# A fixed task list replaced by another: threshold attention and a GELU layer on one Trainium2 core

## The chip, the cores and the metric

The kernel runs on one core of a Trainium2 chip. The metric is the device time of one execution in microseconds (us); less is better. The core's engines each run their own queue of instructions in order: PE (matrix products), DVE (VectorE), ACT (ScalarE), POOL (GpSimd) and SP (SyncE, which here only issues transfers). They wait for one another by semaphores.

## The reference

Attention in which a score counts only if it lies within `tau` of its row's maximum, then two dense layers with a sigmoid-weighted activation between them. q, k and v are 8 x 8 x 576 x 64, `x` is 4608 x 512, the weights 512 x 2048 and 2048 x 512. The weights arrive as float64.

```
scores = scale * np.matmul(q, k.transpose(0, 1, 3, 2))
thresh = np.max(scores, axis=-1, keepdims=True) - tau
scores = np.where(scores >= thresh, scores, -1000000000.0)
scores = scores - np.max(scores, axis=-1, keepdims=True)
attn = np.exp(scores)
attn = attn / (np.sum(attn, axis=-1, keepdims=True) + 1e-09)
x = np.matmul(attn, v)            # (B, H, S, D), then as (B*S, H*D)
h = x @ w_in
g = h * (1.0 / (1.0 + np.exp(-1.702 * h)))
return (g @ w_out)
```

## The kernel before, in words

**Attention.** The 64 heads are handled as 32 pairs n. For each pair, scores are 9 pieces of PE work (`scores_run n,[j]`, line 733), which ACT copies to SBUF (`keep n,j`, L750) into 5 tiles, four of 1152 columns and one of 576. DVE finds maxima in groups (`in_groups`, L773; `over_tiles`, L782), ACT and DVE join the halves (`cross_max` L793, `over_halves` L800, `turn_rows` L808/809), and the row goes through DRAM by GpSimd (`row_out` L825, `row_in` L834), which also adds it to some tiles in the transfer itself (`add_row n,t` L840); DVE does it for others (`sub n,t` L855). ACT then runs `mask n,t` (L862) and `exps n,t` (L866). PE multiplies with v (`values n,tiles`, L877; the first pairs' sums also by PE, `sums_by_pe`), DVE and ACT form the sums (`in_groups` again, `cross_sums` L932, `turn_sums` L937 to 941), they go by DRAM (`sums_out`, `sums_in`, L946, L953), and DVE divides and writes the result into x (`place_x n`, L988).

**The layers.** x is taken in 18 blocks of 256 tokens. Block 0's first layer is plain: `mm1_0 j,i` (L1074, j = 0 to 15), `tanh j` on ACT (L1031), `gelu_0 j` on DVE (L1080), the texts' `gelu j`. Its second layer, and both layers of the later blocks, take 7 products of halves instead of 8 (`product blk,x`, L1619; `read`, L1634 and 1641). Block 0's `product 0,0` needs sums of `w_out` that `t_whole` (DVE, L1204) and `t_minus` (ACT, L1200) form after the last weight piece. PE has 40 small fillers, `stay_warm x` (L1685).

**The weights.** 32 pieces of 512 KB, 0 to 15 of `w_in` and 16 to 31 of `w_out`, are sent for by SP (`load_w i`, L651) and converted on the core: `cv_power i` and `cv_power2 i` on ACT (L661, L665), `cv_whole i` and `cv_end i` on DVE (L679, L686). The raw pieces share a few staging places. Piece 28 takes that of 27, piece 29 that of 23, piece 30 that of 24 and piece 31 that of 30: each load waits for the `cv_end` of the piece before it. SP's transfers also use 8 semaphores in turn, so each waits for the landing of the eighth before it.

**What sets the order.** The builder makes 4767 tasks with their dependencies, and then runs them in the order of `ORDER`, a list of 4767 task numbers on lines 290 to 490. The order of one engine's tasks in this list is the order of its queue; the pools (PSUM banks, score places) are taken in it too. `run_in_order` (L492) walks it:

```
for i in map(int, ORDER):
    x_free.extend(x_used.pop(key) for key in x_ends.get(i, ()) if key in x_used)
    tasks[i][3](*tasks[i][4])
```

Of the kernel before, what the change touches and what calls it, by code (L numbers as in the profile page):

```python
# [32 lines left out]
def kernel(  # L33
# [249 lines left out]
    def transfer(by, time, a, kind=0, give=(), lag=1.7):  # L283
# [7 lines left out]
        192 193 199 195 197 200 196 201 198 268 202 270 269 0 271 6 1 205 264 206 207 7 275 208  # L291
        266 209 265 277 211 210 194 214 212 12 267 216 2 213 18 219 13 215 383 217 221 379 4 220
        224 3 19 274 381 222 225 223 226 24 276 384 229 30 8 380 318 36 218 227 287 382 301 230
        308 385 320 25 319 228 323 14 42 289 321 48 315 231 325 324 31 232 328 9 322 330 326 310
        298 329 203 37 317 327 331 333 233 282 280 335 332 386 284 304 334 43 338 336 234 235 295 389
        339 54 15 291 340 49 286 60 32 279 236 66 285 391 303 307 38 281 452 337 204 390 237 341
        26 294 312 454 392 302 342 299 55 46 393 238 343 344 316 395 239 345 394 398 448 61 396 283
        52 346 400 33 5 403 399 40 305 22 401 293 67 405 450 242 27 288 313 404 300 245 408 406
        453 410 243 455 314 64 309 449 34 306 240 248 297 347 451 251 397 20 272 409 358 252 348 10
        411 407 246 459 362 359 35 241 458 402 244 72 273 253 16 412 56 254 249 17 39 255 11 21  # L300
        256 28 247 349 363 250 73 257 352 350 258 355 50 460 259 41 353 260 70 413 261 351 461 311
        414 278 23 354 669 366 415 262 51 78 670 367 84 356 416 665 368 53 79 44 263 90 417 462
        29 96 369 85 667 357 418 464 419 463 420 666 465 467 364 423 469 91 360 370 426 468 371 470
        97 671 361 429 472 421 387 668 372 471 365 373 672 76 473 466 422 474 388 374 88 102 475 375
        376 424 477 479 432 103 478 523 456 82 480 476 425 296 482 435 481 483 427 457 436 484 57 485
        437 428 58 377 438 486 59 439 433 487 488 430 378 489 440 62 675 490 524 431 94 736 676 434
        441 63 738 737 68 443 65 491 442 677 445 739 69 678 45 446 502 492 681 679 444 740 682 100
        683 506 680 503 80 686 741 742 684 292 447 687 688 81 108 691 493 114 689 693 692 696 694 496
        525 494 507 530 499 497 531 695 495 532 743 498 690 510 500 109 511 685 697 512 71 501 115 698
        120 513 504 699 673 746 514 121 508 505 515 83 811 118 674 700 747 47 516 509 112 813 701 702  # L310
        748 518 124 74 703 106 126 749 812 520 92 517 704 75 521 519 814 86 752 750 744 77 127 753
        522 754 116 757 751 755 526 758 807 527 745 756 93 533 705 534 110 809 759 130 535 762 95 716
        760 706 764 808 536 763 767 761 765 720 537 717 104 528 766 105 538 768 529 87 769 111 107 541
        117 707 98 721 539 770 542 99 113 708 540 101 545 771 810 710 132 543 138 718 133 544 144 546
        772 711 89 773 139 709 713 549 774 722 119 775 547 145 817 550 150 723 712 548 884 151 728 553
        551 724 886 719 885 714 552 554 776 727 128 887 715 557 142 787 725 777 555 129 558 726 788 122
        146 148 729 818 123 131 559 136 819 147 125 821 820 560 824 156 822 778 162 157 730 290 888 825
        134 827 781 826 830 890 163 828 154 152 831 556 833 135 823 836 889 832 834 837 137 153 891 839
        160 838 731 842 158 829 843 732 164 561 791 140 733 835 159 779 562 792 166 894 734 840 141 149
        565 958 165 841 735 563 959 789 566 167 564 844 168 161 782 169 569 143 567 155 174 793 845 180  # L320
        175 780 570 568 960 847 783 784 815 181 573 170 795 848 574 961 571 849 962 796 790 816 171 850
        572 851 794 172 577 846 575 964 852 182 963 178 183 173 184 785 965 578 185 576 186 786 798 187
        853 581 176 797 579 864 854 177 582 580 799 865 188 179 585 583 800 190 801 584 189 586 802 191
        803 593 589 868 804 587 594 869 590 866 595 805 867 596 895 806 855 601 602 588 591 603 870 592
        871 607 896 856 604 858 597 608 598 605 609 859 606 599 612 611 857 610 613 999 861 860 600 615
        872 862 873 616 863 614 998 897 618 874 1000 898 900 899 876 903 901 875 904 1001 906 905 877 909
        907 878 910 912 879 911 915 902 913 880 916 918 908 917 619 919 881 617 921 914 922 882 1003 892
        620 968 923 1002 883 924 622 920 893 1004 926 623 1005 621 927 925 625 928 929 930 939 626 624 943
        931 933 628 932 627 936 940 629 934 947 935 636 633 1007 937 637 630 635 944 632 1006 1200 638 634
        640 938 1202 1201 941 948 969 631 1203 942 970 972 975 971 1196 949 973 976 945 978 1197 974 977 981  # L330
        979 946 982 980 984 983 987 985 950 988 951 990 986 989 993 952 994 966 991 953 641 639 995 992
        954 955 996 643 1198 967 1164 642 1165 644 956 1199 1166 1167 647 1168 957 1177 1171 1181 648 1169 1178 1170
        646 1008 1174 650 1172 649 645 1175 651 1182 1185 1173 653 1206 1176 1009 997 1179 1207 1272 1186 1180 1208 1268
        1273 1210 1213 1209 1211 1214 652 1183 1187 1216 1215 1219 1217 1212 1184 1220 1222 1221 1269 1225 1188 1223 1226 1224
        1228 1227 1231 1229 1218 1232 1204 654 1233 1189 1230 1190 656 1270 1205 1234 1236 1274 1191 1237 657 655 1192 1271
        659 1238 1239 1028 1011 1275 658 1249 1240 660 1010 1193 1030 1253 1243 1250 1241 1242 1035 1194 1031 1032 1278 1029
        1195 661 1036 1033 1344 1246 662 1254 1034 1346 1039 663 1244 1038 1247 1041 1012 1257 664 1040 1251 1043 1345 1042
        1248 1045 1235 1245 1255 1258 1279 1252 1280 1282 1281 1285 1283 1259 1013 1256 1286 1288 1287 1284 1291 1289 1292 1347
        1260 1294 1293 1261 1297 1295 1298 1296 1340 1300 1299 1303 1301 1037 1304 1290 1047 1305 1341 1046 1306 1044 1302 1262
        1048 1452 1308 1453 1014 1309 1050 1049 1310 1311 1057 1052 1263 1321 1015 1264 1054 1312 1053 1342 1325 1322 1051 1058  # L340
        1315 1276 1055 1265 1313 1318 1059 1064 1056 1060 1065 1326 1314 1061 1066 1343 1068 1063 1266 1067 1062 1069 1316 1454
        1277 1329 1323 1071 1016 1324 1456 1070 1350 1267 1072 1327 1331 1317 1455 1416 1075 1319 1074 1307 1320 1073 1351 1330
        1352 1354 1353 1357 1355 1328 1017 1358 1360 1359 1332 1363 1361 1333 1364 1362 1366 1365 1457 1369 1367 1356 1334 1370
        1372 1368 1371 1375 1373 1376 1335 1076 1377 1374 1336 1412 1378 1078 1380 1417 1348 1077 1381 1018 1079 1337 1413 1382
        1383 1081 1080 1349 1418 1393 1384 1082 1397 1387 1394 1385 1414 1386 1390 1419 1084 1019 1338 1388 1401 1085 1391 1083
        1389 1087 1103 1086 1398 1392 1105 1402 1395 1415 1104 1110 1396 1020 1106 1107 1399 1089 1111 1400 1339 1108 1090 1109
        1422 1091 1114 1092 1113 1659 1423 1379 1661 1424 1021 1426 1425 1660 1403 1429 1427 1430 1662 1404 1432 1431 1405 1435
        1433 1022 1406 1436 1434 1023 1438 1088 1437 1024 1441 1439 1663 1428 1442 1444 1665 1440 1443 1447 1445 1448 1420 1115
        1664 1446 1116 1449 1666 1112 1450 1118 1627 1117 1421 1407 1628 1093 1120 1094 1119 1629 1630 1408 1095 1631 1640 1122
        1121 1409 1634 1644 1632 1641 1123 1633 1025 1410 1125 1635 1124 1411 1636 1096 1127 1097 1645 1126 1669 1098 1132 1129  # L350
        1637 1731 1099 1128 1648 1735 1130 1133 1638 1670 1131 1134 1732 1451 1671 1135 1736 1673 1639 1136 1676 1138 1139 1733
# [2416 lines left out]
```

## Time and profile before

| what | value |
|---|---|
| median of 3 runs | 1212.37 us (1211.54 to 1212.95) |
| profiled execution | 1211.57 us |
| its span on the core | 1209.5 us, so 2.07 us lie around it |
| busy: PE, DVE, ACT, POOL | 1192.7, 1062.4, 790.0, 131.3 us |
| PE's granted clock | 1.00 in every stretch |
| span up to `product 0,0` on PE | 172.55 us |

Busy times are of the profiled execution, as are all positions below, in us from the start of its span. PE's share of 99% is a mean: up to 172.5 us the attention of the first pairs, the conversion of the weights and block 0's first layer run on all engines at once, and behind it PE has nearly no gap.

### The profile page before, as it was taken

The page shows a single profiled execution, that of the slowest core. Times are in us where ns is not written, and L with a number is a line of the kernel's source. Part 1 is how long each engine was busy: PE and PEld are TensorE (multiplying, and loading weights), DVE is VectorE, ACT ScalarE, POOL GpSimd, SP SyncE. Part 2 cuts the span into 40 slices and gives each one's busy share as a digit, 9 for nine tenths or more (in the row PEclk, how much of TensorE's full clock was granted, in tenths as well). Part 3 has the DMA queues.
Part 4 walks back from the last instruction along what each step waited for, and adds up shares of the span by engine and source line. Part 5 has one row for each costly group of instructions (what it writes and reads, how often), then busy time and mean ns, then how long its engine had stood idle before and what let it go on. Part 6 is the DMA issues. An engine that isn't in the chain of part 4 may idle for free.

```text
span 1209.5 us, 26132 instructions
## 1 busy us (share of the span) xinstructions
PE 1192.7 (99%) x10560; PEld 980.6 (81%) x10560; DVE 1062.4 (88%) x1622; ACT 790.0 (65%) x1183; POOL 131.3 (11%) x176
## 2 busy tenths in 40 slices
PE   8899999999999999999999999999999999999998
PEld 6556777788877777777777777777778999999998
DVE  6999998989899889998898778997886798799797
ACT  7999986878686779678875568667872340340340
POOL 0122232110001110021100110111100000000000
PEclk9999999999999999999999999999999999999999
DMA  9967778696555655557645644557624544454433
GB/s 263 219 144 191 176 140 167 132 173 191 134 130 129 170 129 116 132 141 179 143 94 119 144 112 102 130 120 181 150 71 132 176 148 141 147 154 137 153 118 114
DMA packets 220616, 176.55 MB, mean 146 GB/s; under 512 B 148752, under 2 KB 165776, under 8 KB 220368
## 3 DMA queue, kind: packets, MB, share of 16 engines
q1 hardware_dynamic: 197776, 125.42, 38.5%
q0 software_dynamic: 22032, 49.17, 20.6%
q8 instruction: 83, 1.36, 0.5%
q10 hardware_dynamic: 688, 0.30, 0.1%
q14 instruction: 37, 0.30, 0.1%
HBM read 119.53 MB, written 25.84 MB: 120 GB/s over the span
## 4 chain that ended last, share of the span: by engine, by line
PE 85%; ACT 8%; DVE 3%; DMA 2%; issue 1%; ACTq 0%; POOL 0%; SPq 0%; DVEq 0%
PE ops L1619 23%; PE pv L877 10%; PE ps L733 9%; PE hps L1311 9%; PE ps L1311 7%; PE ops L1575 6%; PE hps L1466 6%; PE ps L1575 5%; PE ps L1466 5%; PE hps L1138 2%; ACT arena L750 2%; PE ps L1138 2%; ACT arena L866 2%; ACT arena L862 2%; DMA arena<-in_moe_w_out_dram 1%; ACT w_in L661 1%
## 5 line engine op out<-in xcount | busy, mean ns | idle before, releaser
L773 DVE TRANSPOSE_TENSOR_REDUCE part<-arena 128x36 f32<-128x1152 f32 (+1 forms) x250 | 294.7, 1209 | 15.7 <-ACT arena L750 9.0
L750 ACT COPY arena<-ps 128x576 f32<-128x576 f32 x288 | 172.2, 646 | 61.5 <-PE ps L733 60.1
L862 ACT ACTIVATE arena<-arena 128x1152 f32<-128x1152 f32 (+1 forms) x160 | 168.5, 1065 | 53.2 <-DVE arena L855 50.9
L866 ACT ACTIVATE arena<-arena,shift 128x1152 f32<-128x1152 f32 (+1 forms) x160 | 183.1, 1161 | 2.1
L733 PE MATMUL ps<-arena 64*64 64x288 f32 x2304 | 173.3, 407 | 6.0 <-ACT arena L750 2.9
L1619 PE MATMUL ops<-w_out,arena 128*128 128x256 f32 x768 | 174.8, 382 | 0.7 <-DVE osb L1641 0.7
L1619 PEld LDWEIGHTS ops<-w_out,arena 128*128 128x128 f32 x768 | 144.1, 190 | 28.1 <-issue 7.5
L877 PE MATMUL pv<-arena 64*64 64x288 f32 x2176 | 159.7, 405 | 0.2 <-ACT arena L750 0.2
L733 PEld LDWEIGHTS ps<-arena 64*64 64x64 f32 x2304 | 82.2, 132 | 66.3 <-ACT arena L750 23.7
L855 DVE TENSOR_TENSOR arena<-arena 128x1152 f32<-128x1152 f32 (+1 forms) x100 | 130.6, 1337 | 1.2
L877 PEld LDWEIGHTS pv<-arena 64*64 64x64 f32 x2176 | 80.7, 133 | 52.8 <-issue 5.6
L1480 ACT COPY arena<-hps 128x512 f32<-128x512 f32 x66 | 38.2, 585 | 121.1 <-PE hps L1466 116.5
L1619 PE MATMUL ops<-arena 128*128 128x256 f32 x464 | 104.3, 379 | 0.0
L848 POOL DMA_DIRECT2D arena<-arena x50 | 54.2, 1317 | 444.1 <-DVE arena L813 262.5
L1619 PEld LDWEIGHTS ops<-arena 128*128 128x128 f32 x464 | 88.0, 190 | 12.8 <-issue 0.9
L763 DVE TRANSPOSE_TENSOR_REDUCE part<-arena 128x72 f32<-128x2304 f32 x25 | 64.2, 2567 | 12.3 <-ACT arena L866 12.2
L793 ACT ACTIVATE other<-red,gap 32x18 f32<-32x18 f32 x100 | 30.7, 307 | 49.5 <-DVE red L782 48.4
L1311 PE MATMUL hps<-xT,w_in 128*128 128x256 f32 x256 | 59.1, 382 | 0.0
L1311 PEld LDWEIGHTS hps<-xT,w_in 128*128 128x128 f32 x256 | 48.0, 190 | 9.4 <-issue 2.6
L1074 PE MATMUL hps<-xT,w_in 128*128 128x256 f32 x232 | 52.0, 382 | 1.7 <-DVE arena L1080 1.6
L1483 DVE TENSOR_TENSOR arena<-ps,arena 128x512 f32<-128x512 f32 x63 | 42.3, 684 | 12.0 <-PE ps L1466 6.4
L1074 PEld LDWEIGHTS hps<-xT,w_in 128*128 128x128 f32 x232 | 43.4, 190 | 10.4 <-DVE arena L1080 3.3
(224 smaller groups left out, 2040.6 us busy)
## 6 DMA issues: line engine op xcount, KB each, us to landing
arena<-in_v_dram SPq DMA_DIRECT2D x128, 144.0 KB
arena<-exu SPq DMA_DIRECT2D x63, 256.0 KB
arena<-ext SPq DMA_DIRECT2D x60, 256.0 KB
arena<-arena POOLq DMA_DIRECT2D x25, 576.0 KB, 5.7
arena<-wrow POOLq DMA_DIRECT2D x48, 256.0 KB, 4.9
arena<-in_k_dram SPq DMA_DIRECT2D x112, 72.0 KB
arena<-in_q_dram SPq DMA_DIRECT2D x112, 72.0 KB
arena<-arena POOLq DMA_DIRECT2D x25, 288.0 KB, 7.2
```

Of the source, the lines that this page charges most:

```text
L733: nc.tensor.matmul(ps[ts(c, KT), h, 0:SH], lhsT=mats[n, 1][ts(h, D), ts(j, KT)], rhs=mats[n, 0][ts(h, D), ts(c, SH)], start=True, stop=True,)
L750: nc.scalar.copy(out=sT[n, t][:, u], in_=pss.pop((n, j))[:, :, 0:SH])
L773: nc.vector.tensor_reduce(out=stats[n, op][:, t * 2 * QB : min(2 * t + 2, NK) * QB], in_=sT[n, t].rearrange("p u h (g d) -> p (u h g) d", ...
L855: engine.tensor_tensor(out=s, in0=s, in1=mbs[n].unsqueeze(1).to_broadcast(list(s.shape)), op=ALU.add if n in BY_DMA or n in NEGATED else A ...
L862: nc.scalar.activation(out=s, in_=s, func=AF.Prelu, alpha=STEEP)
L866: nc.scalar.activation(out=s, in_=s, func=AF.Exp, scale=SCALE, bias=shift)
L877: nc.tensor.matmul(o[c][ts(h, D), 0:SH], lhsT=left(j, h)[ts(c, KT)], rhs=sT[n, t][ts(c, KT), u, h, :], start=(j == 0), stop=(j == NK - 1),)
L1074: nc.tensor.matmul(hidden[j][:, ts(i, BLK)], lhsT=w_in[:, c, ts(j, P)], rhs=xTs[i][:, c, :], start=(c == 0), stop=(c == NDC - 1), skip_gro ...
L1311: nc.tensor.matmul(o[:, ts(j, BLK)], lhsT=left[:, c, ts(j, P)], rhs=right[:, c, :], start=(x in (P1, P2, P5) and j + c == 0), stop=(j + c ...
L1466: nc.tensor.matmul(o[:, ts(j, HT)], lhsT=left[:, ts(j, P)], rhs=right, start=(m in (P1, P2, P5) and j == 0), stop=(j == 3), skip_group_che ...
L1575: nc.tensor.matmul(banks3[pos, r][:, 0:HT], lhsT=left[:, j, :], rhs=right[:, j, :], start=(m in (P1, P2, P5) and j == 0), stop=(j == 3), s ...
L1619: nc.tensor.matmul(banks[blk][k][:, ts(o, HM)], lhsT=left[:, j, :], rhs=right[:, j, :], start=(j == 0), stop=(j == HF - 1),)
```

## The change

Only the numbers in `ORDER` change: lines 291 to 489, 199 lines of numbers. The tasks, their costs, their dependencies and all functions stay. As described, the list was sought anew with the landing times of GpSimd's transfers and of the last weight piece taken from the trace. The first line of it stands for the rest:

```
     ORDER = """
-        192 193 199 195 197 200 196 201 198 268 202 270 269 0 271 6 1 205 264 206 207 7 275 208
+        192 193 195 199 197 196 200 201 198 268 202 270 269 0 271 6 1 205 264 206 207 7 275 208
...
```

How the queues differ: of 1161 tasks on PE 219 stand at another place, of 1055 on ACT 505, of 1394 on DVE 1018, of 133 on POOL 13 and of 461 on SP 322. Mostly neighbours change places. Three places on DVE matter for what follows.

The first is DVE's queue around the end of piece 27's conversion. L686 is `cv_end`, L679 `cv_whole`, L1080 `gelu`, L773 `in_groups`, L697 the preparation of a pair's q and k. Before, the first `cv_end` here is piece 24's and the second, behind `in_groups 6,3`, is piece 27's; `gelu 8` follows.

```order
L679 TENSOR_SCALAR arena<-arena 128x512
L697 STREAM_TRANSPOSE arena_90<-arena_90 128x1152
L686 SCALAR_TENSOR_TENSOR w_out<-arena,w_out 128x512
L773 TENSOR_REDUCE part<-arena_90 128x36
L686 SCALAR_TENSOR_TENSOR w_out<-arena,w_out 128x512
L1080 SCALAR_TENSOR_TENSOR arena<-xT_94,hps 128x512
L686 SCALAR_TENSOR_TENSOR w_out<-arena,w_out 128x512 x2
L686 SCALAR_TENSOR_TENSOR w_out<-w_out 128x512
```

Now the row of one `cv_end` is piece 23's, `gelu 6` follows it, and then two rows in one, of pieces 24 and 27.

```order
L773 TENSOR_REDUCE part<-arena_90 128x36
L697 STREAM_TRANSPOSE arena_90<-arena_90 128x1152
L679 TENSOR_SCALAR arena<-arena 128x512
L686 SCALAR_TENSOR_TENSOR w_out<-arena,w_out 128x512
L1080 SCALAR_TENSOR_TENSOR arena<-xT_94,hps 128x512
L686 SCALAR_TENSOR_TENSOR w_out<-arena,w_out 128x512 x2
L773 TENSOR_REDUCE part<-arena_90 128x18
L773 TENSOR_REDUCE part<-arena_90 128x36
```

`in_groups 6,3` (the later 128x36 row) moved behind `cv_end 27`, and `cv_end 23` ahead of it.

The second is DVE's queue around piece 30 and `gelu 10`. Before, `gelu 10` (L1080) stands behind `turn_rows 6` (L808, L809), then `cv_whole 28`, the four parts of `place_x 4` (L988), `cv_whole 29`, `cv_end 28`, `cv_whole 30` and `cv_end 30`.

```order
L808 STREAM_TRANSPOSE flat_78<-flat_77 128x32
L809 TENSOR_SCALAR flat_78<-flat_78 128x32
L1080 SCALAR_TENSOR_TENSOR arena<-xT_94,hps 128x512
L679 TENSOR_SCALAR arena<-arena 128x512
L988 TENSOR_TENSOR xT_93<-pv,arena_90 128x192
L988 TENSOR_TENSOR xT_95<-pv,arena_90 128x96
L988 TENSOR_TENSOR xT_95<-pv,arena_90 128x160
L988 TENSOR_TENSOR xT_96<-pv,arena_90 128x128
L679 TENSOR_SCALAR arena<-arena 128x512
L686 SCALAR_TENSOR_TENSOR w_out<-arena,w_out 128x512
L679 TENSOR_SCALAR arena<-arena 128x512
L686 SCALAR_TENSOR_TENSOR w_out<-arena,w_out 128x512
```

Now `cv_whole` 29 and 28 stand ahead of `turn_rows 6` (just above these rows), `cv_end 25` and `cv_whole 30` ahead of `gelu 10`, and behind `place_x 4` follow `cv_whole 26`, a short `in_groups` and `cv_end 30`.

```order
L808 STREAM_TRANSPOSE flat_78<-flat_77 128x32
L809 TENSOR_SCALAR flat_78<-flat_78 128x32
L686 SCALAR_TENSOR_TENSOR w_out<-w_out 128x512
L679 TENSOR_SCALAR arena<-arena 128x512
L1080 SCALAR_TENSOR_TENSOR arena<-xT_94,hps 128x512
L988 TENSOR_TENSOR xT_93<-pv,arena_90 128x192
L988 TENSOR_TENSOR xT_95<-pv,arena_90 128x96
L988 TENSOR_TENSOR xT_95<-pv,arena_90 128x160
L988 TENSOR_TENSOR xT_96<-pv,arena_90 128x128
L679 TENSOR_SCALAR arena<-arena 128x512
L773 TENSOR_REDUCE part<-arena_90 128x18
L686 SCALAR_TENSOR_TENSOR w_out<-arena,w_out 128x512
```

So `cv_whole 30` moved from behind `gelu 10` and `place_x 4` to ahead of both.

The third is DVE's queue around piece 31 and `gelu 13`. Before, `cv_whole 31` (L679) is followed by `gelu 13`, then `turn_sums 5` (L937 to L941), `cv_end 31` and the four `t_whole`.

```order
L686 SCALAR_TENSOR_TENSOR w_out<-arena,w_out 128x512
L782 TENSOR_REDUCE red<-part 128x18
L679 TENSOR_SCALAR arena<-arena 128x512
L1080 SCALAR_TENSOR_TENSOR arena<-xT_94,hps 128x512
L937 SCALAR_TENSOR_TENSOR red<-red,other_84 128x18
L940 RECIPROCAL flat_s_79<-red 128x18
L941 STREAM_TRANSPOSE flat_s_80<-flat_s_79 128x32
L686 SCALAR_TENSOR_TENSOR w_out<-arena,w_out 128x512
L1204 TENSOR_TENSOR w_out<-w_out 128x4x256 x2
L1204 TENSOR_TENSOR arena<-w_out 128x1024 x2
```

Now `gelu 13` follows `cv_end 31`.

```order
L686 SCALAR_TENSOR_TENSOR w_out<-arena,w_out 128x512 x2
L679 TENSOR_SCALAR arena<-arena 128x512
L937 SCALAR_TENSOR_TENSOR red<-red,other_84 128x18
L940 RECIPROCAL flat_s_79<-red 128x18
L941 STREAM_TRANSPOSE flat_s_80<-flat_s_79 128x32
L686 SCALAR_TENSOR_TENSOR w_out<-arena,w_out 128x512
L1080 SCALAR_TENSOR_TENSOR arena<-xT_94,hps 128x512
L1204 TENSOR_TENSOR w_out<-w_out 128x4x256 x2
L1204 TENSOR_TENSOR arena<-w_out 128x1024 x2
```

`gelu 13` moved from ahead of `turn_sums 5` and `cv_end 31` to behind them.

On ACT, the queue near the last pieces was `cv_power 31`, `tanh 13`, `cross_sums 5`, `cv_power2 31`; now it is `tanh 12`, `tanh 13`, `cv_power2 29`, `cv_power 31`, `cross_sums 5`, `cv_power2 31`. `cv_power 30` stands ahead of `cv_power 28` and `tanh 11`, where it stood behind both. On POOL `add_row 6,4` stands ahead of `sums_out 5`. On PE the first half of `product 0,3` stands behind the last parts of `values 6` and `scores_run 7`, where it stood ahead of them. On SP pieces 4 and 5 are sent for ahead of pair 2's q and k, and v of pair 0 later.

396 rows, old and new, of the table ORDER are left out of this document.

## The prediction

> **What bounds the kernel now.** I read the windows of the trace first, because the page's 99% for PE is a mean over unlike stages. The columns are the stretch, its length, then busy time and instructions of PE, PE's weight loads, DVE, ACT and POOL, the granted clock, the DMA engines' share and GB/s.
>
> ```profile
> 0.00:50.00 50.00, 44.85 (x714) 30.58 (x716) 39.35 (x58) 42.93 (x67) 7.88 (x23) 1.00 0.97 246
> 50.00:100.00 50.00, 45.17 (x632) 26.19 (x636) 46.00 (x81) 49.50 (x70) 7.23 (x10) 1.00 0.71 161
> 100.00:150.00 50.00, 49.13 (x369) 37.36 (x362) 49.48 (x70) 49.74 (x77) 13.07 (x18) 1.00 0.77 188
> 150.00:172.50 22.50, 20.87 (x145) 15.86 (x143) 20.01 (x34) 17.59 (x25) 9.16 (x13) 1.00 0.68 144
> 172.50:1206.30 1033.80, 1032.70 (x8716) 870.61 (x8712) 907.30 (x1383) 630.25 (x948) 93.94 (x113) 1.00 0.57 139
> 1206.30:1209.50 3.20, 0.00 (x0) 0.00 (x0) 0.25 (x1) 0.00 (x0) 0.00 (x0) 1.00 0.23 76
> ```
>
> From 172.5 to 1206.3 PE is idle for 1033.80 − 1032.70 = 1.10 us, and 3.20 us follow the last matmul. The list moves no work off PE, so behind 172.5 at most 1.10 us is to be won. Ahead of it ACT is busy for 49.50 and 49.74 of 50 us while PE idles: ACT sets the pace there, and a new order leaves it the same work. What can shift is the moment at which the second layer starts, `product 0,0`. So I read next the chain of waits up to it (start, length, engine and line):
>
> ```profile
> 142.71 0.57 DVE w_out L686
> 143.28 0.60 DVE arena L1080
> ...
> 145.58 8.40 DMA arena<-in_moe_w_out_dram
> 153.98 0.02 issue
> 154.00 0.79 ACT w_out L661
> ...
> 154.81 0.73 ACT w_out L665
> ...
> 155.57 0.70 DVE w_out L686
> ...
> 156.29 6.02 DMA arena<-in_moe_w_out_dram
> ...
> 162.34 0.02 ACT w_out L661
> ...
> 163.02 0.59 ACT xT L1031
> ...
> 163.63 0.70 DVE arena L1080
> ...
> 164.37 3.72 PE hps L1074 x16
> 168.09 4.53 PE pv L877 x72
> 172.62 3.43 PE ops L1619 x15
> ```
>
> Weight piece 30 is sent for at 145.58 and lands at 153.98. ACT and DVE convert it in three steps, and only then is its staging place free for piece 31, which leaves at 156.29 and lands at 162.31. On ACT `tanh 13` stands behind the conversion of piece 31, `gelu 13` follows it on DVE, and `mm1_0 15` follows that on PE at 164.37. From there PE runs without a gap. PE's own view says what this is worth (start, busy time; in brackets the idle time before it and its cause):
>
> ```profile
> 152.77 3.72 PE L1074 MATMUL hps<-xT,w_in 128*128 128x256 f32 x16 [0.92 <-DVE arena L1080]
> 156.91 7.17 PE L1074 MATMUL hps<-xT,w_in 128*128 128x256 f32 x32 [0.42 <-DVE arena L1080]
> 164.37 3.72 PE L1074 MATMUL hps<-xT,w_in 128*128 128x256 f32 x16 [0.28 <-DVE arena L1080]
> ```
>
> The three gaps, ahead of `mm1_0` 12, 13 and 15, make 0.92 + 0.42 + 0.28 = 1.62 us: all that a faster handling of the last pieces can give.
>
> **The change, part by part.** *Sending for piece 30.* SyncE's load of piece 28 waits until DVE has ended the conversion of piece 27, whose staging place it takes; 29 and 30 leave behind it.
>
> ```profile
> 141.34 1.37 DVE L773 TRANSPOSE_TENSOR_REDUCE part<-arena 128x36 f32<-128x1152 f32 x1
> 142.63 0.65 DVE L686 SCALAR_TENSOR_TENSOR w_out<-arena,w_out 128x512 int32<-128x512 int32 x1
> 143.20 0.68 DVE L1080 SCALAR_TENSOR_TENSOR arena<-xT,hps 128x512 f32<-128x512 f32 x1
> ...
> 152.03 0.68 DVE L1080 SCALAR_TENSOR_TENSOR arena<-xT,hps 128x512 f32<-128x512 f32 x1
> 152.63 0.42 DVE L679 TENSOR_SCALAR arena<-arena 128x512 int32<-128x512 uint32 x1
> 152.97 0.94 DVE L988 TENSOR_TENSOR xT<-pv,arena 128x192 f32<-128x192 f32 x4
> 153.83 0.42 DVE L679 TENSOR_SCALAR arena<-arena 128x512 int32<-128x512 uint32 x1
> ```
>
> ```profile
> 143.31 2.69 SPq L651 DMA_DIRECT2D arena<-in_moe_w_out_dram  x3
> ```
>
> `cv_end 27` is the second row, and load 28 leaves 0.03 us behind its end (142.63 + 0.65 = 143.28). In the new list `in_groups 6,3` (142.63 − 141.34 = 1.29 us to the next start), `cv_end 22` (0.57, as the row at 142.63) and `cv_whole 26` (0.34, as the row at 152.63) no longer stand ahead of it, and `cv_end 23` (0.57) does: 1.29 + 0.57 + 0.34 − 0.57 = 1.63 us earlier, about 141.7. Load 29, which waited for `cv_end 23`, no longer waits, so 30 can leave some 0.8 us behind 28, at 142.5. When it lands the trace bounds from both sides. By its own 8.40 us it lands at 150.9. If instead the three loads of one go (2.69 us in the SyncE row) share what bandwidth there is, the 153.98 − 143.31 = 10.67 us from load 28 to the landing of 30 stay, and it lands at 152.4. I take the middle, 151.65, since both rows describe the same transfer.
>
> [...]
>
> *What waits for it.* In the new list `cv_whole 30` stands ahead of `gelu 10` on DVE, and `cv_power 30` ahead of `cv_power 28` and `tanh 11` on ACT. Before, `gelu 10` ran at 152.03 with piece 30 still under way; now it waits for the landing, call it L. Queued behind it on DVE are `place_x 4`, `cv_end 30` and `gelu 11`, and PE waits for them. `cv_whole` takes 0.34 to the next start, `gelu` to PE's start 152.77 − 152.03 = 0.74: `mm1_0 12` starts at L + 1.08 = 152.73, against 152.77.
>
> *Sending for piece 31.* Up to `cv_end 30` DVE now has, behind L, `cv_whole 30` 0.34, `gelu 10` 0.60, `place_x 4` 0.86 (152.97 to 153.83), `cv_whole 26` 0.34, a short `in_groups` and `cv_end` 0.57. The short one is this row, 0.69 to the next start:
>
> ```profile
> 145.62 0.76 DVE L773 TRANSPOSE_TENSOR_REDUCE part<-arena 128x18 f32<-128x576 f32 x1
> 146.31 0.64 DVE L1080 SCALAR_TENSOR_TENSOR arena<-xT,hps 128x512 f32<-128x512 f32 x1
> ```
>
> That is 3.40; ACT's three conversions need less and are hidden. With 0.1 us of issue, load 31 leaves at L + 3.5 = 155.15 (before: 156.29) and, at 6.02 us, lands at L + 9.5 = 161.2 (before: 162.31).
>
> *From piece 31 to PE.* `tanh 13` now runs ahead of the wait, but `gelu 13` has moved on DVE from ahead of `turn_sums 5` and `cv_end 31` to behind them. So PE's next operands wait for the whole conversion, where before they waited for its first step:
>
> ```profile
> 163.62 0.42 ACT L932 COPY other<-red 32x18 f32<-32x18 f32 x2
> 164.07 0.72 ACT L665 ACTIVATE w_out<-w_out,rebias 128x512 int32<-128x512 f32 x1
> ```
>
> `cv_power 31` 0.68 (163.02 − 162.34), `cross_sums 5` 0.45 (164.07 − 163.62), `cv_power2 31` 0.74 with its issue, `cv_end 31` 0.57, `gelu 13` to PE 0.74: 3.18 us behind the landing, where before it was 164.37 − 162.31 = 2.06. `mm1_0 15` starts at L + 9.5 + 3.2 = L + 12.7 = 164.35, against 164.37: what the earlier piece brings, 1.1 us, is spent by the longer way. With L = 150.9 it is 163.6 (−0.8), with 152.4 it is 165.1 (+0.7).
>
> *Behind 172.5.* `product 0,3,(0, 4)` moves behind the last `values 6` and `scores_run 7`, next to its second half, which saves PE a change between 64*64 and 128*128 tiles and back.
>
> ```profile
> 191.03 1.99 PE L1619 MATMUL ops<-w_out,arena 128*128 128x256 f32 x8
> 192.95 0.71 PE L877 MATMUL pv<-arena 64*64 64x288 f32 x8
> 193.49 0.67 PE L733 MATMUL ps<-arena 64*64 64x288 f32 x8
> 194.08 1.99 PE L1619 MATMUL ops<-w_out,arena 128*128 128x256 f32 x8
> 195.91 3.62 PE L1619 MATMUL ops<-arena,arena 128*128 128x256 f32 x16
> ```
>
> Alone in its tile size a half takes 192.95 − 191.03 = 1.92 to the next start; inside a run of its size it is (199.37 − 195.91)/2 = 1.73, and last before a like one 195.91 − 194.08 = 1.83. The values take 0.54 behind a change and about 0.49 in a run. So (1.92 − 1.73) + (0.54 − 0.49) = 0.24 us go. The one stall here keeps its cause, since `place_x 6` keeps its place ahead of the read:
>
> ```profile
> 199.37 3.62 PE L1619 MATMUL ops<-arena,xT 128*128 128x256 f32 x16
> 203.68 6.53 PE L1619 MATMUL ops<-w_out,arena 128*128 128x256 f32 x29 [0.69 <-DVE osb L1641]
> ```
>
> GpSimd's `add_row 6,4` passes `sums_out 5`, about 1 us later for the latter; `place_x 5`, its reader, has also moved back, behind `gelu 15`. I put the price at 0, with ends of −0.7 (that stall gone) and +0.7 (another of its size). The other moves ahead of 150 (keeps, exps, conversions, loads of q, k, v) lie under ACT's full queue: 0, with ends of −0.76 (all of ACT's idle time from 50 to 150, 0.50 + 0.26) and +0.9 (a PE gap as long as the longest above).
>
> *The sum.* 0.0 (start of `product 0,0`) − 0.24 + 0 = −0.24 us. The profiled execution took 1211.57 us, its span 1209.5 with 2.07 around it; it would take 1211.3. The median of the runs is 1212.37, and on that footing the forecast is 1212.1. A measurement of this kernel tells no less than about 0.2%, 2.4 us, from no change, so this is no change.
>
> **The rivals.** *Piece 30 lands no earlier (slower).* Sent for earlier, it shares the DMA engines with what else is queued, whose share from 100 to 150 is already 0.77, and lands between 153.98 as before and, with the same 1.6 us of other loads put ahead of it, 155.6. For it: 8.40 us for a piece that takes 6.02 when alone. Against it: the share leaves room. `gelu 10` and load 31 now hang on the landing, so all is later by L − 151.65: `mm1_0 15` at 166.7 to 168.3, +2.3 to +3.9, less 0.24: 1214.4 to 1216.0, middle 1215.2. It decides from L of about 152; beyond the measurable bound from L = 154.3. [...]
>
> *Earlier start (faster).* The three gaps (1.62) and ACT's idle time from 50 to 150 (0.76) go altogether, with the 0.24: −2.6, 1209.8. For it: ACT's wait of over 2 us for piece 31 is time its queue could use. Against it: the new way behind piece 31 is longer.
>
> *A new stall in the long stretch (slower).* A late transfer on the reordered SyncE or GpSimd queues stops PE for as long as the 3.20 us behind the last matmul, the nearest wait for a transfer with PE idle: 1215.3. Against it: 1.10 us of idle in 1033.80, so there is slack before.
>
> *The clock.* The fillers `stay_warm` move, and PE's longest gap ahead of 172.5 may grow.
>
> ```profile
> 57.77 1.26 PE L733 MATMUL ps<-arena 64*64 64x288 f32 x16 [2.02 <-ACT arena L750]
> ```
>
> This gap left the clock at 1.00. [...]
>
> **How the numbers follow.** Forecast (L from 150.9 to 152.4, stalls unlike by 0.7): 0.60. Late piece 30: 0.20, of which 0.08 lies under the measurable bound. Earlier start: 0.15. New stall: 0.05. So faster 0.15, same 0.60 + 0.08 = 0.68, slower 0.12 + 0.05 = 0.17. The forecast's own range is −0.24 with −0.8 −0.7 −0.76 and +0.7 +0.7 +0.9 at their ends, 1209.9 to 1214.4. To hold 8 in 10 the range reaches a little beyond the faster case and to the middle of the late one: 1209.4 to 1215.4.
>
> **What would show it.** Right: load 28 leaves near 141.7 and piece 30 lands near 151.7; `mm1_0 12` starts near 152.7, load 31 leaves near 155.2, ACT runs `tanh 13` ahead of piece 31, `mm1_0 15` near 164.4, `product 0,0` near 172.5; PE idle behind it stays near 1.1 us. Wrong: a landing of piece 30 past 154 with DVE idle ahead of `cv_whole 30`, a gap on PE behind 172.5 of over 1 us, or ACT done so early that `product 0,0` starts before 171.

## The result, and the profile after

The new list takes 1210.34 us (median of 20 runs, 1209.08 to 1212.30), the old one 1212.45 us (20 runs, 1210.52 to 1214.25): a ratio of 0.9984, with a 95% interval from 0.9977 to 0.9991. That is 2.1 us or 0.16% less: a small gain that 20 runs resolve, under the bound of 0.2% and inside the stated range. The profiled execution took 1209.3 us, its span 1207.2, against 1211.57 and 1209.5.

The windows of the profile after, cut at the same places:

```profile
0.00:50.00 50.00, 44.77 (x720) 33.12 (x724) 38.76 (x59) 42.55 (x66) 8.07 (x23) 1.00 0.92 255
50.00:100.00 50.00, 44.59 (x632) 26.17 (x628) 47.55 (x80) 49.76 (x71) 7.01 (x10) 1.00 0.66 156
100.00:150.00 50.00, 49.02 (x370) 38.20 (x363) 49.44 (x73) 49.75 (x78) 13.35 (x19) 1.00 0.84 198
150.00:172.50 22.50, 21.75 (x150) 16.96 (x149) 22.38 (x35) 20.17 (x28) 9.82 (x13) 1.00 0.59 125
172.50:1204.00 1031.50, 1030.88 (x8708) 870.52 (x8706) 904.33 (x1380) 626.80 (x945) 93.04 (x112) 1.00 0.56 139
1204.00:1207.20 3.20, 0.00 (x0) 0.00 (x0) 0.28 (x1) 0.00 (x0) 0.00 (x0) 0.98 0.28 88
```

From 150 to 172.5 PE is idle for 0.75 us instead of 1.63, and behind that for 0.62 instead of 1.10. DVE is busy for 22.38 of these 22.50 us, where it was 20.01: it hardly waits any more. The chain of waits says the same. It has no transfer of a weight piece in it now:

```profile
150.03 0.42 DVE arena L679
...
158.65 0.58 DVE arena L1080
...
159.27 3.72 PE hps L1074 x16
...
163.01 3.72 PE hps L1074 x16
166.73 4.53 PE pv L877 x72
171.26 8.83 PE ops L1619 x40
```

PE's view of the same place:

```profile
146.72 11.82 PE L1074 MATMUL hps<-xT,w_in 128*128 128x256 f32 x54
159.27 7.46 PE L1074 MATMUL hps<-xT,w_in 128*128 128x256 f32 x32 [0.73 <-DVE arena L1080]
```

The bracketed gaps ahead of `mm1_0` 12, 13 and 15 are gone; one of 0.73 us ahead of `mm1_0 14` is new. SyncE's view shows when pieces 28 to 30, and 31, are sent for:

```profile
141.81 1.29 SPq L651 DMA_DIRECT2D arena<-in_moe_w_out_dram  x3
...
153.53 0.35 SPq L651 DMA_DIRECT2D arena<-in_moe_w_out_dram  x1
```

Load 28 leaves at 141.81, as forecast (141.7). By the updates of the transfers' semaphores piece 30 lands at 148.94, 2.7 us ahead of the forecast, and piece 31, sent for at 153.53, at 158.78. DVE does not wait for either (no brackets):

```profile
150.03 0.42 DVE L679 TENSOR_SCALAR arena<-arena 128x512 int32<-128x512 uint32 x1
150.37 0.68 DVE L1080 SCALAR_TENSOR_TENSOR arena<-xT,hps 128x512 f32<-128x512 f32 x1
...
160.68 0.42 DVE L679 TENSOR_SCALAR arena<-arena 128x512 int32<-128x512 uint32 x1
```

The first row is `cv_whole 30`, 1.1 us behind the landing, the second `gelu 10`, the last `cv_whole 31`, 1.9 us behind its landing. Further on PE's view shows `product 0,3` in one piece and no stall ahead of `product 0,6` (201.12; the four rows follow each other without a bracket):

```profile
190.66 3.72 PE L1619 MATMUL ops<-w_out,arena 128*128 128x256 f32 x16
194.21 3.62 PE L1619 MATMUL ops<-arena,arena 128*128 128x256 f32 x16
197.67 3.62 PE L1619 MATMUL ops<-arena,xT 128*128 128x256 f32 x16
201.12 8.80 PE L1619 MATMUL ops<-w_out,arena 128*128 128x256 f32 x40
```

Where the 2.27 us between the two ends of PE's work (1206.22 and 1203.95) lie, by the starts of four instructions in PE's and ACT's records:

| stretch | before | after | difference |
|---|---|---|---|
| span start to ACT's first `keep` | 8.99 | 9.43 | +0.44 |
| to `mm1_0 8` | 128.77 | 128.12 | -0.65 |
| to `product 0,0` | 34.78 | 33.64 | -1.14 |
| to `product 0,6` | 31.13 | 29.93 | -1.20 |
| to the end of the last matmul | 1002.55 | 1002.83 | +0.28 |

### The profile page after: what moved, and what is told of

Same layout as the page of the kernel before. It is cut to its first block, busy times and chain, and to the rows that moved or that the text cites. A ratio compares the mean times of both kernels' runs of the same rounds, so it can differ in the third digit from the quotient of the medians.

```text
span 1207.2 us, 26125 instructions
## 1 busy us (share of the span) xinstructions
PE 1191.0 (99%) x10560; PEld 985.0 (82%) x10560; DVE 1062.7 (88%) x1622; ACT 789.0 (65%) x1183; POOL 131.3 (11%) x176
## 4 chain that ended last, share of the span: by engine, by line
PE 87%; ACT 8%; DVE 3%; DMA 1%; issue 0%; ACTq 0%; DVEq 0%
PE ops L1619 24%; PE pv L877 10%; PE ps L733 10%; PE hps L1311 9%; PE ps L1311 7%; PE ops L1575 6%; PE hps L1466 6%; PE ps L1575 5%; PE ps L1466 4%; PE hps L1138 2%; ACT arena L750 2%; PE ps L1138 2%; ACT arena L866 2%; ACT arena L862 2%; PE hps L1074 1%; ACT w_in L661 1%
## 5 line engine op out<-in xcount | busy, mean ns | idle before, releaser
L773 DVE TRANSPOSE_TENSOR_REDUCE part<-arena 128x36 f32<-128x1152 f32 (+1 forms) x250 | 295.9, 1211 | 20.0 <-ACT arena L750 11.4
L1641 DVE SCALAR_TENSOR_TENSOR osb<-ops,osb 128x256 f32<-128x256 f32 x84 | 33.7, 414 | 19.3 <-PE ops L1619 17.7
```

Of the source, the lines that this page charges most:

```text
L773: nc.vector.tensor_reduce(out=stats[n, op][:, t * 2 * QB : min(2 * t + 2, NK) * QB], in_=sT[n, t].rearrange("p u h (g d) -> p (u h g) d", ...
```

## The experiments

Since both lists hold the same tasks at three cuts (behind places 591, 812 and 914), each list can be spliced from the two. Times are given as ratios to the kernel before on the same chip; the stretches of the table above come from the one profile of each run.

**The old list again.**

> The kernel before once more, unchanged, for a second profile of it: how far the landing times of the weight pieces and the start of product 0,0 differ from one execution to the next. Theory (the order decides): piece 30 lands within 1 us of 153.98, product 0,0 starts within 0.5 us of 172.55, and the 0.69 us stall near 203 is there again. Rival (the difference of the two profiles is that of two executions): piece 30 lands 2 us or more elsewhere, or product 0,0 starts 1 us or more elsewhere.

Stretches: 128.81, 34.05, 30.66, 1002.72. Piece 30 landed at 153.60, so 0.4 us earlier, and piece 31 3.9 us behind its issue instead of 6.0; `product 0,0` started at 172.11. By the bounds set, the theory holds for the landing and for `product 0,0` (0.44 us off), but not for the stall ahead of `product 0,6`, of which 0.22 us are there instead of 0.69:

```profile
202.76 3.50 PE L1619 MATMUL ops<-w_out,arena 128*128 128x256 f32 x15 [0.22 <-DVE osb L1641]
```

The landing and the start stay under the rival's bounds, yet between these two executions of one list the middle differs by 0.73 us and the third stretch by 0.47. The old middle, behind the old opening and with DVE's and ACT's old order, was profiled four times more (here and in three runs below) and took 34.03 to 34.09 us, against 34.78 in the first profile. Of the 1.14 us some 0.4 are therefore the list's, and 0.7 belong to one execution of the old one.

**The middle stretch of the new list alone** (places 592 to 812), twice.

```diff
-places 592 to 812 of the old list
+places 592 to 812 of the new list
```

> The list before, with its places 592 to 812 (from mm1_0 5 to just ahead of product 0,0, about 119 to 171 us) taken from the new list; all else as before. Theory: the earlier start of product 0,0 comes from this stretch alone: it starts near 171.2 us (before 172.55), piece 30 lands near 149 and not near 154, PE's gaps ahead of mm1_0 12 and 13 are gone, time -1.4 us, perhaps less the stall at 203 as well. Rival (the new first stretch, up to 119 us, brings it): product 0,0 stays within 0.3 us of 172.55.

> The same list as in the run with places 592 to 812 of the new one alone, once more. There the stretch from mm1_0 8 to product 0,0 was 33.80 us (old list 34.0 to 34.8), yet the median was 1.5 us above the kernel before, with the first copy on ACT at 11.4 us instead of 9.0 and a half-speed window of PE's clock at 60 us. Theory (the late start and the clock window come by chance with each execution): the median is within 1.0 us of the kernel before or below it, and where the profile starts near 9.0 to 9.4 us, product 0,0 is near 171.6. Rival (this list itself starts late): again 1 us or more above, and again a first copy near 11.4.

The ratio was 1.0008 (0.9999 to 1.0017), then 1.0005 (0.9996 to 1.0014): not faster. Yet the stretch itself took 33.81 and 33.66 us, about as in the new list, with the gaps ahead of `mm1_0` 12 and 13 gone, though piece 30 landed at 151.32 and 151.10 and not near 149. What is lost lies around it. In the first, ACT's first `keep` came at 11.37, in the second at 9.88, so the late start did not come back in full, and the second median (0.6 us above the kernel before) is within the bound of the theory of chance; 9 and 7 of 11 runs were over 1212 us. In the second, the unchanged third stretch took 31.54, with this stall ahead of `product 0,6` on PE:

```profile
204.47 1.78 PE L1619 MATMUL ops<-w_out,arena 128*128 128x256 f32 x7 [1.11 <-DVE osb L1641]
```

And in both profiles, PE's clock fell. The windows of the first, and in PE's view the gap ahead of it:

```profile
60.50:63.90 3.40, 3.40 (x36) 1.97 (x32) 3.40 (x4) 3.40 (x6) 0.00 (x0) 0.50 0.86 201
```

```profile
60.12 1.90 PE L733 MATMUL ps<-arena 64*64 64x288 f32 x16 [2.02 <-ACT arena L750]
```

For 3.4 us the granted clock is 0.50 (in the second profile from 60.0 to 63.3 us); sixteen matmuls take 1.90 us that take 1.26 in the profile before. The stretch to `mm1_0 8` took 129.12 and 129.39 us, 0.3 and 0.6 more than without it.

**The third stretch alone** (places 813 to 914).

```diff
-places 813 to 914 of the old list
+places 813 to 914 of the new list
```

> The list before, with its places 813 to 914 (product 0,0 to just ahead of product 0,6, about 171 to 203 us) taken from the new list. Theory: one change between tile sizes fewer on PE, -0.24 us between the starts of product 0,0 and product 0,5, and the stall of 0.69 us ahead of product 0,6 goes, because ACT now makes both w_copy 0 about 1 us earlier and GpSimd's 1 MB transfer w_plus 0, behind which sums_out 6 is queued, ends earlier: -0.9 us in all. Rival (the stall goes only because all before it is earlier): -0.24 us and the stall stays at 0.6 us or more.

0.9990 (0.9981 to 0.9998); from `product 0,0` to `product 0,6` 29.96 us, as in the new list (29.93), without a stall. The theory holds for the size; its reason is tested further down.

**The opening and the end alone** (places 1 to 591, and 915 on).

```diff
-places 1 to 591 and 915 to 4767 of the old list
+places 1 to 591 and 915 to 4767 of the new list
```

> The new list's places 1 to 591 (up to about 119 us) and 915 to the end (from product 0,6), with the two stretches between them as before. Theory: ACT sets the pace up to 119 us and PE has no gap in the last stretch, so nothing changes: product 0,0 within 0.3 us of 172.55, time within 0.5 us. Rival (the early loads and copies gain): product 0,0 earlier by 0.7 us or more.

0.9992 (0.9983 to 1.0001), no clear time. But the stretch to `mm1_0 8` took 128.12 us, exactly as in the new list's profile, 0.65 less than before; the last stretch took 1002.56, so the new end gives nothing. The theory of no change falls for the opening. In this profile the gain was lost in the middle: with piece 30 landing at 154.99, the old middle took 35.70 us, with these gaps on PE:

```profile
153.00 3.72 PE L1074 MATMUL hps<-xT,w_in 128*128 128x256 f32 x16 [1.10 <-DVE arena L1080]
157.92 10.63 PE L1074 MATMUL hps<-xT,w_in 128*128 128x256 f32 x48 [1.20 <-DVE arena L1080]
```

PE's earlier start meets later pieces here: piece 27 landed at 137.76 and load 28 left at 144.11, against 135.5 to 135.7 and 143.3 to 143.6 in the two profiles of the old list. Whether the new opening makes them late or this execution did is not shown by one profile.

**Sending piece 30 early, in the old list.**

```diff
 DVE: ... prep 7
+cv_end 23
 cv_end 24
-in_groups 6,3
 cv_end 27
+in_groups 6,3, cv_end 22, cv_whole 26
```

> The list before with one step of the new one: on DVE cv_end 23 stands ahead of cv_end 24, and in_groups 6,3, cv_end 22 and cv_whole 26 stand behind cv_end 27; so loads 28, 29 and 30 leave about 1.6, 3 and 3 us earlier. Theory (the earlier sending alone): load 28 near 141.9, piece 30 lands near 149 to 150 instead of 153.4 to 154; gelu 10 stays at 152.0 and mm1_0 12 at 152.8, since DVE's queue sets them; cv_end 30 and gelu 11 lose their wait of 0.4 us, load 31 leaves 0.5 us earlier: product 0,0 0.3 to 0.7 us earlier, not 1.1 to 1.4. Rival (the sending is all): the stretch from mm1_0 8 to product 0,0 falls to the 33.6 to 33.8 us of the new list (34.0 to 34.8 before).

1.0007 (0.9997 to 1.0016); the stretch took 35.55 us, 0.8 to 1.5 more than in the old list. Both theories fall: DVE now waits 2.02 us for ACT's `cv_power2 23`, which the old order of ACT has later, and load 28 leaves at 144.31, later than before. (Piece 30 still landed at 150.45, 5.3 us behind its issue.)

```profile
142.39 1.90 DVE L686 SCALAR_TENSOR_TENSOR w_out<-arena,w_out 128x512 int32<-128x512 int32 x3 [2.02 <-ACT w_out L665]
```

**DVE's queue of the middle alone.**

```diff
-DVE, places 592 to 812: old order
+DVE, places 592 to 812: new order
 ACT: old order, but
-cv_power 28, cross_max 6, tanh 10, exps 5,3, cv_power2 28
+cross_max 6, tanh 10, exps 5,3, cv_power 28, cv_power2 28
```

> The list before with only DVE's queue of the stretch from 119 to 171 us from the new one (and cv_power 28 on ACT moved behind exps 5,3, without which that queue can't run); ACT, SyncE, GpSimd and PE as before. Theory: DVE's queue carries the gain of this stretch: from mm1_0 8 to product 0,0 33.6 to 33.9 us. Rival (ACT's queue is as much of it): 34.2 us or more.

1.0054 (1.0038 to 1.0071): slower by 6 us, the stretch took 40.12. The theory falls; the rival had the side, but not the size. Without ACT's queue, DVE waits for it at one place after another, and PE for DVE:

```profile
145.28 3.72 PE L1074 MATMUL hps<-xT,w_in 128*128 128x256 f32 x16 [1.74 <-DVE arena L1080]
150.19 10.63 PE L1074 MATMUL hps<-xT,w_in 128*128 128x256 f32 x48 [1.19 <-DVE arena L1080]
...
171.77 3.72 PE L1074 MATMUL hps<-xT,w_in 128*128 128x256 f32 x16 [1.88 <-DVE arena L1080]
```

So DVE's queue does not give the gain without ACT's; ACT's queue without DVE's was not run.

**Piece 30 later, in the new list**, first behind transfers of q and k, then behind those of v as well.

```diff
 SyncE: load_w 28, load_w 29
-load_w 30
 load_qk 8,0,1, load_qk 8,1,0
+load_w 30            (first run)
 load_v 6
+load_w 30            (second run)
```

> The new list with one step moved: on SyncE the load of piece 30 stands two pairs of transfers later (behind 8,0,1 of q and 8,1,0 of k), so that it leaves near 146.5 instead of 142.7 and lands, at 6.2 us, near 152.7 instead of 148.9. Theory (the late-piece rival of the prediction, whose price is L - 151.65): gelu 10 on DVE waits for the landing, mm1_0 12 starts at L + 1.1 = 153.8 instead of 151.5, mm1_0 15 at L + 12.7 = 165.4 instead of 163.0, product 0,0 at about 173.5 instead of 171.2: +2.3 us. Rival (the new list no longer hangs on piece 30): product 0,0 within 0.5 us of 171.2.

The ratio was 0.9979 (0.9970 to 0.9988), the middle 33.73 us: within 0.1 us of the new list's. Load 30 left 3.3 us later, at 145.95, and by the updates of its semaphore landed at 151.04: a flight of 5.1 us, not the 6.2 I had counted, so the theory's landing near 152.7 did not come about. `cv_whole 30` is the second row; it starts just as the piece has landed and the row before it has ended (150.36 + 0.69):

```profile
150.36 0.69 DVE L686 SCALAR_TENSOR_TENSOR w_out<-w_out 128x512 int32<-128x512 int32 x1
151.06 0.45 DVE L679 TENSOR_SCALAR arena<-arena 128x512 int32<-128x512 uint32 x1
```

So the run does not test the price of a late piece. It shows that the 1.1 us between the landing and `cv_whole 30` in the new list are slack. `product 0,0` started at 172.06, 0.9 us later than in the new list's profile, because `mm1_0 8` had started 0.8 us later; counted from there, the rival holds. (The next expectation takes the flight here for 2.2 us; what landed at 148.14 was a transfer of q, sent at 143.61.)

> The new list with the load of piece 30 moved further back on SyncE, behind the four transfers of v for pair 6, so that it leaves near 150.3 and lands between 152.5 (2.2 us, as when it left near 146 behind landed pieces) and 155. Theory (L is what counts, once it is late enough): mm1_0 12 at L + 1.1 or later, mm1_0 15 at L + 12.7, so the stretch from mm1_0 8 to product 0,0 35 to 37 us instead of 33.6 to 33.7. Rival (DVE's queue, not the landing, sets this stretch in the new list, with 3 us of slack and more): it stays within 0.3 us of 33.7.

Now it landed at 155.34, 5.1 us behind its issue; the stretch took 39.75 us, more than the theory's 35 to 37, and the time was 1217.19 us (one run).

```profile
150.29 0.58 SPq L651 DMA_DIRECT2D arena<-in_moe_w_out_dram  x1
...
158.87 0.35 SPq L651 DMA_DIRECT2D arena<-in_moe_w_out_dram  x1
```

```profile
155.37 0.43 DVE L679 TENSOR_SCALAR arena<-arena 128x512 int32<-128x512 uint32 x1 [3.62 <-DMA arena<-in_moe_w_out_dram]
```

```profile
156.45 12.31 PE L1074 MATMUL hps<-xT,w_in 128*128 128x256 f32 x48 [3.18 <-DVE arena L1080]
170.75 3.72 PE L1074 MATMUL hps<-xT,w_in 128*128 128x256 f32 x16 [1.99 <-DVE arena L1080]
```

`cv_whole 30` waits for the landing, `mm1_0 12` starts at L + 1.11 (forecast 1.08), load 31 leaves at L + 3.53 (forecast 3.5): these two steps of the prediction stand to 0.03 us. `mm1_0 15` comes at L + 15.4 and not 12.7, since piece 31 took 8.5 us (158.87 to 167.39), not 6.0. (PE also ran at half speed from 157.1 to 160.5, so the 48 matmuls took 12.31 us, where 48 take 10.63 in the rows of two runs above; `mm1_0 15` still waits for `gelu 13`, which starts at 170.02.) The late-piece rival was a real mechanism; its condition was not met.

**Two copies on ACT together, in the old list.**

```diff
 ACT: w_copy 0,1
+w_copy 0,0
 exps 6,1, mask 6,2, exps 6,2
-w_copy 0,0
```

> The list before with one step moved: on ACT w_copy 0,0 stands directly behind w_copy 0,1, so that GpSimd's 1 MB transfer w_plus 0 leaves near 181 instead of 184.5; all else as before. Theory (sums_out 6 is queued behind that transfer, and lands when it ends): sums_in 6 on GpSimd leaves 2.5 us or more earlier than at 196.3, and the stall of 0.3 to 0.7 us ahead of product 0,6 goes: from product 0,0 to product 0,6 30.2 to 30.4 us instead of 30.7 to 31.1. Rival (the small transfer's own landing time decides): sums_in 6 within 0.7 us of 196.3 and the stall stays.

0.9991 (0.9982 to 1.0000); 30.42 us, with 0.15 of the stall left. GpSimd's `w_plus 0` left at 179.41 instead of 184.47, but landed at 191.32, hardly ahead of the 191.94 of the old list run again. `sums_in 6` left at 193.58 (196.29 in the profile before, 194.16 in the old list again). So of the expected 2.5 us most was that first profile's own lateness: against the second, it is 0.6. The reason given is not shown.

**Half of `product 0,3` behind `values 6`, in the old list.**

```diff
 PE: scores_run 7,[7]
-product 0,3,(0, 4)
 values 6,[4], scores_run 7,[8]
+product 0,3,(0, 4)
 product 0,3,(4, 8)
```

> The list before with one step of the new one: on PE the first half of product 0,3 stands behind the last parts of values 6 and scores_run 7. Theory: this one move is the gain behind product 0,0. It saves a change of tile size there and back (0.24 us), and since values 6 ends 2.1 us earlier, SyncE's load of v for pair 7, which waits for that, leaves 2.1 us earlier (19.0 instead of 21.1 us behind product 0,0) and no longer shares the DMA engines with GpSimd's sums_in 6, which lands 3.5 to 3.8 us after it leaves instead of 4.7 to 5.1; place_x 6 is in time and the stall ahead of product 0,6 goes: from product 0,0 to product 0,6 29.9 to 30.1 us (old list 30.3 to 31.3). Rival (the other moves of this stretch, the copies on ACT and the sums on DVE, take the stall away): -0.24 us, and a stall of 0.3 us or more stays in a run in which sums_in 6 leaves with the load of v.

29.93 us, no stall: this one move is the whole gain of the third stretch. SyncE's load of v for pair 7 leaves at 192.75, 19.0 us behind `product 0,0`; in all eight profiles with that half where it was, it was 21.13. `place_x 6` on DVE, which waits for the sums:

```profile
199.71 0.95 DVE L988 TENSOR_TENSOR xT<-pv,arena 128x192 f32<-128x192 f32 x4 [0.47 <-DMA arena<-row_s]
```

It starts 3.95 us behind the issue of `sums_in 6`; in the seven with the old place where it left within 1.3 us of v's load, 4.7 to 5.8 us, and 3.7 in the first profile, where it left 2.6 us behind that load. By the updates of its semaphore the second of the two transfers of the sums landed 4.0 to 5.1 us behind its issue in those seven, and 2.9 to 3.3 in the other seven of the fourteen profiles. So the load of v beside it is what delays the sums. The time was 0.9993 (0.9984 to 1.0002), so the move is seen in the trace and not told from nothing in the median. The profiled run also had a half-speed window (0.50 from 14.0 to 17.4 us), and its opening took 130.69 us.

**Two `gelu` earlier, in the new list.**

```diff
 DVE: cv_end 28
+gelu 12
 in_groups 5,2
-gelu 12
 over_tiles 5, cv_end 26, cv_end 29
+gelu 13
 cv_whole 31, turn_sums 5, cv_end 31
-gelu 13
```

> The new list with two steps moved on DVE: gelu 12 ahead of in_groups 5,2, and gelu 13 back ahead of cv_whole 31 (where the list before had it ahead of cv_end 31). Theory (in the new list PE's gap of 0.73 to 0.83 us ahead of mm1_0 14 is DVE's order alone, and nothing else is late): the gap goes, from mm1_0 8 to product 0,0 32.9 to 33.0 us instead of 33.6 to 33.7, time -0.7 us against the new list. Rival (the wait moves on: gelu 14, tanh 15 or the sums of w_out are late next): 33.4 us or more.

0.9993 (0.9984 to 1.0001): it does not beat the new list (0.9984 and, with piece 30 moved, 0.9979). The middle took 33.30 us, 0.34 less instead of 0.73: `gelu 12` now waits 0.94 us for ACT's `tanh 12`, and 0.51 us of the gap stay. The sums of `w_out` are later for it, and the third stretch took 30.94 us: 0.6 us are lost up to `product 0,5`, most of it ahead of `product 0,2`, where PE waits for ACT, and 0.4 in the stall again. By its bound (33.4 us) the rival narrowly fails, but what it names happened: the wait moved on.

```profile
159.11 0.69 DVE L1080 SCALAR_TENSOR_TENSOR arena<-xT,hps 128x512 f32<-128x512 f32 x1 [0.94 <-ACT xT L1031]
```

## Why the prediction was right, and where not

**The size.** "No change" by the bound of 0.2% was right; but the 0.24 us forecast was a ninth of the 2.1 us measured, and 20 runs of each list tell that from nothing. Three terms came out at or beyond their fast ends, which the range was wide enough to hold: the number was right, partly by luck, and much of the working behind it was not. Of the signs named, load 28 at 141.7 and `tanh 13` ahead of piece 31 came; `mm1_0 12` (151.47), load 31 (153.53), `mm1_0 15` (163.01) and `product 0,0` (171.19) all came 1.2 to 1.7 us ahead of theirs.

**Sending for piece 30** was right: 141.81 against 141.7. **The landing L was the step that failed.** I took 151.65, between an own flight of 8.40 us and a fixed 10.67 us from load 28; it was 148.94. Both rows came from a list in which load 29 had waited for `cv_end 23` and left 1.9 us behind load 28. In all six profiles with that wait, piece 30 was in flight for 7.6 to 8.6 us; in the six in which loads 28, 29 and 30 left together, 5.3 to 6.7 us; in the two in which it left 2.8 us or more behind load 29, 5.1 us. So the flight goes with the order of the sending, and I carried it from one order into another. Why a later load 29 makes piece 30 slower is not shown; what leaves behind it is hardly the reason, for the run that sends piece 30 early keeps the old queue of SyncE and has a flight of 5.3 us. The 6.02 us of piece 31 weren't those of a piece alone either: a transfer of k had left 0.9 us ahead of it and one of GpSimd's followed after 0.5, and over the fourteen profiles it took 3.9 to 8.5 us.

With L below DVE's arrival at `cv_whole 30` (150.03) the landing no longer decides; DVE's queue does, busy for 22.38 of 22.50 us, and the run with two `gelu` earlier moves PE's gaps by that queue alone. A balance like the one I drew came about all the same, but on DVE and not by the piece. By the starts of PE's groups, against the old list run again, 1.09 and 0.52 us are won ahead of `mm1_0` 12 and 13, and 0.79 and 0.29 lost ahead of 14 and 15. So the middle gave 0.4 us against the usual old execution (34.05 to 33.64), 1.14 against the profiled one.

**From piece 31 to PE**: the longer way behind the landing is there (`gelu 13` at 162.28, behind `cv_end 31`), and it costs the 0.29 us just named, not the 1.1 us forecast: `mm1_0 15` starts 0.73 us behind `gelu 13` and 3.74 us behind `mm1_0 14`, where a group of 16 without a wait follows after 3.45. PE's view has no bracket there, because such a group is listed with 3.72 us and so overlaps the next by 0.27. For the same reason the three gaps of the prediction, 1.62 us by their brackets, were 1.09 + 0.70 + 0.45 = 2.24 us by the starts.

**Behind 172.5** the saving for the tile sizes was 0.34 us, not 0.24: from `product 0,0` to `product 0,5` it took 26.82 us in all eight profiles with the half where it was, and 26.48 in the new list. I put the stall at 0 because `place_x 6` keeps its place; that was the second failing step. I had counted the moved half of the product for PE alone. What hangs on `values 6`, which it passed, is SyncE's load of v for pair 7, and with it the landing of the sums. The run with only this move shows the stall gone: some 0.4 us (median; 0 to 1.3 over seven profiles of the old third stretch, by the time from `product 0,5` to `product 0,6`) on top of 0.34.

**The opening** I put at 0 with an end of -0.76. In three of five profiles with the new opening it took 128.12 to 128.17 us, in two 128.9 and 129.0, where ACT's copy at 14.4 us came some 0.7 us later; in the five old ones without a half-speed window 128.76 to 128.84. So it gave 0.65 us in three profiles and nothing in two. Which of its moves gives it was not tried.

**The clock** I put into no term of the sum, since the 2.02 us gap had left it at 1.00. That was one execution's luck. Four of nine profiles with the old opening have a half-speed window of 3.4 us in it, three of them at the 2.02 us gap; none of the five with the new one has, whose longest gap is 1.78 us. The traces show where the chance lies. The changes of the granted clock in one profile lie on a grid of 3.413 us: two of them are 1204.905 us apart in the profile before, 353 such steps, and 1201.491 us in the one after, 352 steps. Its place against the span's start differs from execution to execution: a step begins at 4.66 us in the first of these, at 5.55 in the second. In the grid step just ahead of the four drops PE was busy for 1.39 to 1.54 us (1.39 in the first run of the new middle alone); of the steps up to 200 us with 1.63 us or more none was followed by a drop, and three between 1.42 and 1.52 were not either (1.51 in the profile before, from 55.86 us). In the old opening the 2.02 us gap leaves 1.39 to 1.41 us of work when it falls inside one step, and more when the grid cuts it; in the new opening no 3.41 us around its longest gap have less than 1.64, wherever the grid lies.

A half-speed window, 0.50 for 3.41 us of some 1210, takes 0.0014 off the mean clock of a run, so a run listed as 1.000 had none. That is so for 50 of 52 runs with the new opening (the one with piece 30 behind v left out) and for 50 of 148 with the old one; 0.998 or less, which needs a window, is listed for 1 and for 47. The others, at 0.999, can be either: the old list run again has 0.999 without a window, from half speed behind the last matmul (the profile after has 0.98 there, over its last 3.20 us). A window costs 0.2 to 0.6 us at 60 us, where ACT sets the pace; the one at 14 us went with 1.9. Of the 79 runs of the old list beside the experiments, the 28 listed as 1.000 have a median 0.6 us under that of all (1211.60 against 1212.22), though on one of the three chips there is no difference.

**The rivals**: the late piece was no case (L 148.94, decisive from 150.0 in the new list), the new stall neither. The faster case (-2.6 us) came out nearest in its total, but not by its terms: the three gaps went and 1.1 us came back at `mm1_0` 14 and 15, and the stall and the clock were not in it. In typical executions the parts add up to 0.4 (middle, 34.05 to 33.64), 0.8 (third, 30.70 to 29.93) and 0.65 (opening, three in five): 1.8 us, with the clock's windows on top, against 2.1 (1.1 to 2.8). That the two spliced lists with the new middle alone came out no faster, though that stretch is shorter in both, stays open: a late start in one profile, a longer stall in the other and the clock's window in both outweigh it there. The window falls where the old opening has its gap, and so goes with the place of the grid; whether that list brings on the late start or it came by chance isn't shown.

## What to carry to other kernels

An order is worth what its weakest pair of queues allows: a better queue on DVE cost 6 us until ACT's came with it, and a better opening was lost in an old middle, in the one profile of it. For a step that moves, ask what is freed by the steps it passes, transfers too; here half a product let a load leave 2.1 us earlier and so took a stall away elsewhere. A transfer's flight time belongs to the order in which it was measured: here it stayed at 7.6 to 8.6 us over six profiles of one order and fell to 5.1 to 6.7 when the loads ahead of it left at other times. And a single profile is a sample: 0.7 of the 1.14 us in the middle were one execution's.

## What the hardware showed that I had not expected

A half-speed window of 3.4 us, at a granted clock of 0.50, came after a PE gap of 2.02 us in some executions of the same opening and not in others. In the step of the 3.413 us grid that held most of that gap PE was busy for 1.39 us in the first run of the new middle alone, where the drop came, and for 1.51 us in the profile before, where it did not; over all profiles the two cases overlap, at 1.39 to 1.54 and 1.42 to 1.52 us. Pieces 28 to 31, of 512 KB each, were in flight for 3.5 to 8.6 us. The first copy on ACT came 8.9 to 11.4 us into the span for openings that are alike, so two runs can differ by 2 us before any change counts:

```profile
11.37 1.18 ACT L750 COPY arena<-ps 128x576 f32<-128x576 f32 x2 [2.79 <-PE ps L733]
```
